# Attention over memory slots and a routed expert: a batch's queries, keys, values and phi laid on 128 partitions, scores on 16 array tiles, and the opening in another order

## The chip, the core and the metric

The kernel runs on one core of one Trainium2 chip. The core has a matrix engine (PE, with its weight loads shown apart as PEld), a vector engine (DVE), an activation engine (ACT), a general engine (POOL), a queue engine (SP) that issues most transfers, and 16 DMA engines. SBUF is the working memory of 128 partitions; PSUM is the matrix engine's output memory, 8 banks of 512 floats a partition. The metric is the device time of one execution in microseconds (us), taken as the median of several runs.

## The reference, cut to what matters

```python
# q, k, v: [8, 8, 576, 64]   phi: [8, 8, 576, 32]   (batch, head, token, ...)
a = softmax(phi over its 32 memory slots)
k_m, v_m = a^T k, a^T v                  # [8, 8, 32, 64]: 32 memory slots per head
attn = softmax(q k_m^T / 8)              # over the 32 slots
x = (attn v_m), heads side by side       # [4608, 512]
logits = x w_gate + modality_bias[modality_id]
e = argmax(logits); gate = softmax(logits)[e]
out = gate * (relu(x w1[e]) w2[e])       # w1: [8, 512, 1024], w2: [8, 1024, 512]
```

## The kernel before

**The work.** The attention never forms x. Since x w1 = attn (v_m w1), the kernel multiplies the 32 value rows of each head into the first expert matrix once per batch (`value_weights`, L604; two halves of 512 columns) and then takes attn times that product as the hidden layer. Large products are taken in a fast 32-bit form with each operand split into a rounded upper part and a remainder; three products (upper by upper, upper by remainder, remainder by upper) stand for one. That gives three matmul lines in `hidden` (L617 to L619) and three terms in `outputs` (L643). One expert is guessed for all tokens from the first token's modality (`guess`, L180); `others` and `verdict` check the guess, and `again` holds the general way, which doesn't run here.

**Per batch** the attention does, in this order: `mem_max`, `mem_top`, `mem_exp` (softmax weights over phi's slots with a shared maximum; DVE, two PE transposes, ACT), `kv_products` and `kv_divide` (L317, L343: keys and values of the slots, and the sums that divide them), `mem_turn` (keys and values transposed through PE, copied out by ACT), `mem_gate` (L421: values times the gate weights), `q_turn` (L432: queries transposed in 32 by 32 blocks by DVE, in place), `scores` (L442), `soften` and `normalise` (softmax over slots, on DVE and ACT), `a_split` (attention weights as upper part and remainder) and `logits`, `gate`. The experts then do `hidden` in two parts per batch (tokens in 4 and 5 of 9 groups), `outputs` for tiles of 128 tokens, and the store.

**Layout.** A batch's 576 tokens are 64 row blocks of 9. Queries lie in `q_sb` with a pair of batches, one on each half of the 128 partitions, all 8 heads side by side. For keys, values and phi a row block is cut in two pieces of 5 and 4 tokens, which lie on neighbouring partitions (`load_keys`, L158); the shorter piece is padded by a column of zeros, or of a very low number for phi. So `kv_products` contracts 128 partitions in 5 steps, for each of two head groups g and four heads j: 40 matmuls on array tiles of 128 rows by 32 columns. `scores` works on one batch's half of the partitions, in two parts: 32 matmuls of 32 by 32 tiles per part, on two of the four row groups of the array. (A matmul of plain 32-bit floats is two rows in the trace: 40 matmuls of the code stand as 80.)

**What sets the order.** Each engine runs its own instructions in program order. `weave` (L903) writes that order: two lists, attention steps and expert steps, each step with the steps that it needs, a due time, and a table of assumed costs (`TAKES`, L688). It takes an attention step when it is due and its inputs should be ready, else the next expert step. All waits are semaphores put in by the framework.

**The opening** is written out in `plan_first` (L745) and at L958 to L989: phi, queries, keys and values of batch 0 are loaded, the matrix engine is kept going by matmuls on zeros (`warm`, L146; 38 at the start, then 4, 26, 6, 6, 3 and 3), and the chain for part 0 of batch 0 runs to its `a_split` (step x0), behind which `hidden` starts. The first half of w1 and of w2 are loaded behind the guess.

**PSUM.** Four banks (`pe`) rotate among the expert products; one bank each is named `pa` and `mem`; two are `sc`, for scores.

Of the kernel before, what the change touches and what calls it, by code (L numbers as in the profile page):

```python
# [53 lines left out]

@with_exitstack
def attn_moe(ctx: ExitStack, tc: tile.TileContext, q, k, v, phi, mod_id, w_gate, mod_bias, w1, w2, out):
    nc = tc.nc
# [7 lines left out]
    KC = 5  # L65
# [15 lines left out]
    LOW = -1e30  # L81
# [11 lines left out]
    def bank(name):  # L93
        return (ps_e if name == "pe" else ps_x).tile([P, 512], F32, name=name)
# [9 lines left out]
    kTs = [const.tile([P, NG, 2, P], F32, name=f"kT{i}") for i in range(4)]  # L104
# [13 lines left out]
    q_sb = big.tile([P, H, QC * D], F32, name="q_sb")  # L118
    kv_sb = big.tile([P, 2, H, KC * D], F32, name="kv_sb")
    phs = [big.tile([P, H, KC * M], F32, name=f"ph{i}") for i in range(2)]  # L120
    raw1 = big.tile([P, KCH, FF], F32, name="raw1")

    raw2 = kv_sb.rearrange("p t h x -> p (t h x)")[:, 0:FCH * DM].rearrange("p (c d) -> p c d", d=DM)
# [29 lines left out]
    def rows_in(src, b, half):  # L153
        r0, r1 = (KC, QC) if half else (0, KC)
        n = src.shape[3]
        return src[b].rearrange("h (p c) d -> p h (c d)", c=QC)[:, :, r0 * n:r1 * n]

    def load_keys(dst, src, b):  # L158

        n = src.shape[3]  # L160
        nc.sync.dma_start(dst[1::2, :, n:KC * n], rows_in(src, b, 1))
        nc.sync.dma_start(dst[0::2, :, :], rows_in(src, b, 0))

    def load_phi(b):
        load_keys(phs[b % 2], phi, b)

    def load_kv(b, t):
        load_keys(kv_sb[:, t], (k, v)[t], b)

    def first_bias():  # L170

        mine = wk.tile([P, E], F32, name="mine")
        live["mine"] = mine
        for m in range(NMOD):
            if m == 0:
                nc.vector.tensor_scalar(mine, mb[:, m], is_m0[m], None, op0=ALU.mult)
            else:
                nc.vector.scalar_tensor_tensor(mine, mb[:, m], is_m0[m], mine, op0=ALU.mult, op1=ALU.add)

    def guess():  # L180

        mine = live.pop("mine")
# [3 lines left out]
        nc.vector.tensor_reduce(fstar, mine, axis=AX.X, op=ALU.max)  # L186
# [53 lines left out]
    def load_queries(pair):  # L240
        for i in range(2):
            nc.sync.dma_start(
                q_sb[QP * i:QP * (i + 1)], q[2 * pair + i].rearrange("h (p c) d -> p h (c d)", c=QC)
            )

    def load_first_queries(b):

        src = q[b].rearrange("h (p c) d -> p h (c d)", c=QC)
        for part in range(2):
            half, c0, n = lies(b, part)  # L250

            (nc.scalar if b == 0 and part else nc.sync).dma_start(
# [856 lines left out]
```

## Time and profile before

| | us |
|---|---|
| median of 3 runs | 421.99 (421.29 to 422.07) |
| the profiled execution's own time | 422.38 |
| its span | 420.6 |
| first matmul of `hidden` (start) | 30.91 |
| first matmul of `outputs` (start) | 39.10 |

The span runs from the first to the last instruction of the profiled execution; 1.8 us of that execution lie around it. A row of the timeline gives start, duration, engine, line, operation, tiles and, in brackets, how long the engine stood idle before it and what ended that. Rows of the same kind next to each other are merged, with their count behind an x. A row of the table of stages (windows) gives the stretch, its length, busy time of PE, PEld, DVE, ACT and POOL with instruction counts, the granted PE clock (1.00 is full speed), the share of the DMA engines' time in use, and GB/s. Ends of matmuls are modelled, so costs on PE are best read from one start to the next.

### The profile page before, as it was taken

The page shows a single profiled execution, that of the slowest core. Times are in us where ns is not written, and L with a number is a line of the kernel's source. Part 1 is how long each engine was busy: PE and PEld are TensorE (multiplying, and loading weights), DVE is VectorE, ACT ScalarE, POOL GpSimd, SP SyncE. Part 2 cuts the span into 40 slices and gives each one's busy share as a digit, 9 for nine tenths or more (in the row PEclk, how much of TensorE's full clock was granted, in tenths as well). Part 3 has the DMA queues.
Part 4 walks back from the last instruction along what each step waited for, and adds up shares of the span by engine and source line. Part 5 has one row for each costly group of instructions (what it writes and reads, how often), then busy time and mean ns, then how long its engine had stood idle before and what let it go on. Part 6 is the DMA issues. An engine that isn't in the chain of part 4 may idle for free.

```text
span 420.6 us, 10080 instructions
## 1 busy us (share of the span) xinstructions
PE 399.8 (95%) x4224; PEld 324.0 (77%) x4224; DVE 243.4 (58%) x575; ACT 150.0 (36%) x355; POOL 36.2 (9%) x66
## 2 busy tenths in 40 slices
PE   8599979999999999999999999999999999989993
PEld 6458877688858979697967878688877889778982
DVE  4566875873778436864685425884588406861400
ACT  1156243433433334442432424343342423431410
POOL 2047400002000200002000200002000200000000
PEclk9869999999999999999999999999999999999998
DMA  7999267983611299617311289431701011341112
GB/s 177 325 351 295 50 164 223 201 306 94 240 27 38 71 295 206 251 27 220 114 27 27 83 286 215 178 100 43 235 13 38 26 27 28 126 152 26 27 27 56
DMA packets 42167, 56.91 MB, mean 135 GB/s; under 512 B 3712, under 2 KB 30336, under 8 KB 42112
## 3 DMA queue, kind: packets, MB, share of 16 engines
q1 hardware_dynamic: 41296, 55.51, 45.4%
q10 hardware_dynamic: 816, 0.66, 0.6%
q8 instruction: 35, 0.57, 0.6%
q14 instruction: 20, 0.16, 0.1%
HBM read 37.29 MB, written 18.87 MB: 134 GB/s over the span
## 4 chain that ended last, share of the span: by engine, by line
PE 86%; DVE 5%; DMA 4%; ACT 3%; issue 1%; ACTq 0%; DVEq 0%
PE pe L643 47%; PE pe L617 8%; PE pe L618 7%; PE pe L619 7%; PE sc L452 5%; PE mem L327 4%; PE pe L594 4%; DMA q_sb<-in_q_dram 3%; PE pa L537 2%; PE mem L138 1%; ACT exp L303 1%; DMA mb<-n_moe_modality_bias_dram 1%; PE pa L150 1%; DVE hl L626 1%; DVE vwl L144 1%
## 5 line engine op out<-in xcount | busy, mean ns | idle before, releaser
L643 PE MATMUL pe<-w2h,hh 128*128 128x512 f32 x288 | 118.2, 411 | 0.0
L643 PE MATMUL pe<-w2h,hl 128*128 128x512 f32 x288 | 112.4, 390 | 0.0
L643 PE MATMUL pe<-w2l,hh 128*128 128x512 f32 x288 | 110.5, 392 | 0.0
L626 DVE SCALAR_TENSOR_TENSOR hl<-pe,hh 128x256 fp32r<-128x256 f32 (+2 forms) x160 | 58.3, 393 | 55.0 <-ACT hh L623 54.3
L643 PEld LDWEIGHTS pe<-w2h,hh 128*128 128x128 f32 x288 | 54.0, 188 | 23.1 <-issue 13.3
L623 ACT ACTIVATE hh<-pe 128x256 fp32r<-128x256 f32 (+2 forms) x160 | 52.9, 362 | 40.3 <-PE pe L619 39.9
L643 PEld LDWEIGHTS pe<-w2l,hh 128*128 128x128 f32 x288 | 54.0, 188 | 12.1
L643 PEld LDWEIGHTS pe<-w2h,hl 128*128 128x128 f32 x288 | 54.2, 188 | 9.2
L656 ACT ACTIVATE ob<-pe,gates 128x512 f32<-128x512 f32 x36 | 24.7, 689 | 71.8 <-PE pe L643 47.7
L617 PE MATMUL pe<-xbh,vwh 128*128 128x320 f32 x128 | 40.1, 313 | 1.6 <-DVE hl L626 1.6
L617 PE MATMUL pe<-xah,vwh 128*128 128x256 f32 x128 | 37.5, 293 | 2.6 <-DVE hl L626 1.8
L618 PE MATMUL pe<-xbl,vwh 128*128 128x320 f32 x128 | 39.5, 309 | 0.0
L619 PE MATMUL pe<-xbh,vwl 128*128 128x320 f32 x128 | 39.5, 309 | 0.0
L618 PE MATMUL pe<-xal,vwh 128*128 128x256 f32 x128 | 36.3, 283 | 0.6 <-DVE xal L144 0.6
L619 PE MATMUL pe<-xah,vwl 128*128 128x256 f32 x128 | 36.1, 282 | 0.0
L267 POOL TENSOR_TENSOR t2sums<-exp 128x512 f32<-128x512 f32 x6 | 7.7, 1284 | 271.1 <-ACT exp L303 271.1
L617 PEld LDWEIGHTS pe<-xah,vwh 128*128 128x128 f32 x128 | 24.4, 191 | 4.9 <-DVE hl L626 2.7
L486 ACT ACTIVATE a<-a 128x640 f32<-128x640 f32 (+2 forms) x17 | 11.2, 657 | 46.5 <-DVE a L485 46.5
L435 DVE STREAM_TRANSPOSE q_sb<-q_sb 128x512 f32<-128x512 f32 (+2 forms) x34 | 23.3, 729 | 4.8 <-DMA q_sb<-in_q_dram 4.8
L617 PEld LDWEIGHTS pe<-xbh,vwh 128*128 128x128 f32 x128 | 24.1, 188 | 2.6 <-DVE hl L626 2.3
L618 PEld LDWEIGHTS pe<-xal,vwh 128*128 128x128 f32 x128 | 24.5, 191 | 1.1 <-DVE xal L144 0.8
L619 PEld LDWEIGHTS pe<-xah,vwl 128*128 128x128 f32 x128 | 24.4, 191 | 0.0
(114 smaller groups left out, 478.5 us busy)
## 6 DMA issues: line engine op xcount, KB each, us to landing
out_dram<-ob SPq DMA_DIRECT2D x64, 128.0 KB, 2.4
q_sb<-in_q_dram SPq DMA_DIRECT2D x6, 1152.0 KB, 11.0
kv_sb<-in_k_dram SPq DMA_DIRECT2D x8, 640.0 KB, 5.9
kv_sb<-in_v_dram SPq DMA_DIRECT2D x8, 640.0 KB, 8.0
kv_sb<-in_k_dram SPq DMA_DIRECT2D x8, 512.0 KB, 5.1
kv_sb<-in_v_dram SPq DMA_DIRECT2D x8, 512.0 KB, 7.0
ph<-in_phi_dram SPq DMA_DIRECT2D x8, 320.0 KB, 3.6
ph<-in_phi_dram SPq DMA_DIRECT2D x8, 256.0 KB, 3.3
```

The lines of the kernel that those rows point to most:

```text
L327: nc.tensor.matmul(kvp[M * j:M * (j + 1), g, :, :], lhsT=pe[:, h, c * M:(c + 1) * M], rhs=kv_sb[:, ts.start:ts.stop, h, c * D:(c + 1) * D] ...
L435: nc.vector.transpose(x, x)
L452: nc.tensor.matmul(to[M * j:M * (j + 1), a], lhsT=kTs[b % 4][p0:p0 + BL, g, u, M * j:M * (j + 1)], rhs=qT[p0:p0 + BL, NG * j + g, c0:c0 + ...
L486: nc.scalar.activation(x, x, AF.Exp, scale=SCALE)
L594: nc.tensor.matmul(pvs[g][M * j:M * (j + 1), :], lhsT=vT[b][rows, j, :], rhs=raw1[rows, j, cols], start=True, stop=True, tile_position=(D ...
L617: nc.tensor.matmul(ph[:, 0:n], lhsT=vh[:, g, cols], rhs=xh, start=(g == 0), stop=False)
L618: nc.tensor.matmul(ph[:, 0:n], lhsT=vh[:, g, cols], rhs=xl, start=False, stop=False)
L619: nc.tensor.matmul(ph[:, 0:n], lhsT=vl[:, g, cols], rhs=xh, start=False, stop=(g == NG - 1))
L623: nc.scalar.activation(hs[0][:, f, h0:h0 + p1 - p0], ph[:, p0:p1], AF.Relu)
L626: nc.vector.scalar_tensor_tensor(hl, ph[:, p0:p1], 0.0, hh.bitcast(F32), op0=ALU.max, op1=ALU.subtract)
L643: nc.tensor.matmul(po, lhsT=tile_columns(hl if n == 1 else hh, f, t), rhs=(w2l if n == 2 else w2h)[:, f, :], start=(f == n == 0), stop=(f ...
L656: nc.scalar.activation(ob, po, AF.Copy, scale=gate_of(b, t))
```

## The change

**Layout.** Queries, keys, values and phi of one batch now lie on 128 partitions: the lower half holds heads of group 0, the upper half those of group 1, with the 64 row blocks of 9 tokens in each half. One transfer fills a tensor of a batch (`halves`); the padding and its fills are gone; `q_sb` is two buffers that take batches in turn.

**Scores** of a whole batch (from batch 1 on) are one step: 32 matmuls of 288 columns, on all four row groups and four column groups of the array, each row group writing its own bank. The four banks are the two pairs `pair0` and `pair1`, into which `pa`, `mem` and `sc` have been merged: `pair0` serves warm matmuls, logits and now `mem_gate`, `pair1` the rest of the memory steps. So scores take both pairs. Batch 0 keeps two steps, of 128 and 160 columns.

**Keys and values:** `kv_products` contracts 64 partitions in 9 steps on tiles of 64 rows by 32 columns, the two head groups side by side: 72 matmuls in place of 40. `mem_top` has one transpose in place of two; `mem_exp` spreads the maximum by two matmuls on 64 columns of the array in place of two transposes; `keys_out` is one ACT copy in place of two or four; the sums of batch 1 go from DVE to POOL, as those of batches 2 to 7 already did.

**Opening:** loads go phi, keys, first 4 query groups, values, last 5 query groups, modality ids, gate weights; then the guess and w1, w2. The values' products of batch 0 are split in two steps, the split of the value weights into upper (ACT) and lower (DVE) steps, and the first four blocks of `hidden` are taken in two passes (two terms, then the third), so that they don't need the lower part at once.

```diff
-    kTs = [const.tile([P, NG, 2, P], F32, name=f"kT{i}") for i in range(4)]
+    kTs = [const.tile([P, 2, P], F32, name=f"kT{i}") for i in range(2)]
...
+    def halves(src, b):
+        return src[b].rearrange("(j g) (p c) d -> (g p) j (c d)", g=NG, c=QC)
     def load_phi(b):
-        load_keys(phs[b % 2], phi, b)
+        nc.sync.dma_start(phs[b % 2], halves(phi, b))
...
-    def kv_products(b, ts, name="mem"):
+    def kv_products(b, ts, banks=None, cs=range(QC)):
...
-            for c in range(KC):
-                for j in range(HG):
-                    h = NG * j + g
+        for c in cs:
+            for j in range(HG):
+                for g in range(NG):
+                    half = slice(QP * g, QP * (g + 1))
                     nc.tensor.matmul(
-                        kvp[M * j:M * (j + 1), g, :, :], lhsT=pe[:, h, c * M:(c + 1) * M],
-                        rhs=kv_sb[:, ts.start:ts.stop, h, c * D:(c + 1) * D],
-                        start=(c == 0), stop=(c == KC - 1), tile_position=(0, M * j),
+                        kvp[g][M * j:M * (j + 1)], lhsT=pe[half, j, c * M:(c + 1) * M],
+                        rhs=kv_sb[half, ts.start:ts.stop, j, c * D:(c + 1) * D],
+                        start=(c == 0), stop=(c == QC - 1), tile_position=(QP * g, M * j),
                     )
...
-    def scores(b, part):
-        half, c0, n = lies(b, part)
-        sc = ps_x.tile([P, 2, 512], F32, name="sc")
-        qT = q_sb.rearrange("p h (c u t) -> p h c u t", u=2, t=BL)
-        for g in range(NG):
-            to = sc[:, :, g * n * BL:(g + 1) * n * BL].rearrange("p a (c t) -> p a c t", t=BL)
-            for u in range(2):
-                for j in range(HG):
-                    for a in range(2):
-                        p0 = QP * half + BL * a
+    def scores(b, c0=0, n=QC):
+        sc = [pair_of_banks(g) for g in range(NG)]
+        qT = q_sb[b % 2].rearrange("p j (c u t) -> p j c u t", u=2, t=BL)
+        cs = slice(c0, c0 + n)
+        for u in range(2):
+            for j in range(HG):
+                for g in range(NG):
+                    for a in range(2):
+                        p0 = QP * g + BL * a
                         nc.tensor.matmul(
...
+                            sc[g][M * j:M * (j + 1), a, c0 * BL:(c0 + n) * BL].rearrange("p (c t) -> p c t", t=BL),
+                            lhsT=kTs[b % 2][p0:p0 + BL, u, M * j:M * (j + 1)], rhs=qT[p0:p0 + BL, j, cs, u, :],
+                            start=(u == 0), stop=(u == 1), tile_position=(p0, M * j),
                         )
...
     def mem_gate(b):
-        pg = bank("mem")
+        pg = bank("pa")
...
-        "s0": (1.05, ""), "s1": (1.25, ""), "e": (0.0, "D1.3 A0.45"), "n": (0.0, "D2.8"),
+        "s0": (0.75, ""), "s1": (0.9, ""), "s": (1.3, ""), "e": (0.0, "D1.3 A0.45"), "n": (0.0, "D2.8"),
...
-        nothing(26)
+        nothing(22)
...
-        add(("x", 0, 0), "x0", [("n", 0, 0, 2)], a_split, 0, 0)
-        add(("vw", 0, 1), "vw", [], value_products, 0, 1, floor=20.7)
-        add(("vws", 0, 1), "nothing", [], value_split, 1)
+        add(("vwu", 0, 0), "vwu", [("vw", 0, 0)], value_upper, 0)
+        add(("vw", 0, 1), "vwp", [], value_products, 0, 1, pair_(1), floor=19.7)
+        add(("x", 0, 0), "x0", [("n", 0, 0, 2)], a_split, 0, 0)
+        add(("vwl", 0, 0), "vwl", [("vwu", 0, 0)], value_lower, 0)
+        add(("vwu", 0, 1), "vwu", [("vw", 0, 1)], value_upper, 1)
+        add(("vwl", 0, 1), "vwl", [("vwu", 0, 1)], value_lower, 1)
...
-                if t == 2 and f == FCH - 1 or t == 3 and f == FCH // 2 - 1:
+                if t == 2 and f == (FCH // 2 if b else FCH) - 1 or t == 3 and f == FCH // 2 - 1:
                     next_values(t - 2)
```

The first place is SP's queue at the start of the program. Before (`ph` is phi, `kv_sb` keys and values, `raw_105` w1; the last query piece of batch 0 is issued from ACT and isn't in this list):

```order
L161 DMA ph_103<-in_phi_dram 64x8x128
L162 DMA ph_103<-in_phi_dram 64x8x160
L252 DMA q_sb<-in_q_dram 64x8x256
L161 DMA kv_sb<-in_k_dram 64x8x256
L162 DMA kv_sb<-in_k_dram 64x8x320
L161 DMA kv_sb<-in_v_dram 64x8x256
L162 DMA kv_sb<-in_v_dram 64x8x320
L188 TENSOR_LOAD star
```

The same place now:

```order
L159 DMA ph_102<-in_phi_dram 128x4x288
L162 DMA kv_sb<-in_k_dram 128x4x576
L166 DMA q_sb_99<-in_q_dram 128x4x256
L162 DMA kv_sb<-in_v_dram 128x4x576
L166 DMA q_sb_99<-in_q_dram 128x4x320
L957 DMA mid<-in_moe_modality_id_dram 64x8x18
L961 DMA wg<-in_moe_w_gate_dram 128x4x8
L190 TENSOR_LOAD star
```

Seven transfers of 64 partitions became five of 128, keys went ahead of the first queries, and modality ids and gate weights, which stood behind w1, went ahead of the guess (`star`).

The second place is PE from the keys' transposes to the scores of batch 1 (`L643` and `L623` are output products, `vT` the transposed values, `wgd` the gate weights). Before:

```order
L138 MATMUL mem<-ident,keys 128x128 x2
L138 MATMUL mem<-ident,values 128x128
...
L643 MATMUL pe<-w2l,hh 128x512
L452 MATMUL sc<-q_sb,kT_78 32x128 x32
L424 MATMUL mem<-wgd,vT_82 32x16 x4
L452 MATMUL sc<-q_sb,kT_78 32x160 x32
```

Now:

```order
L623 MATMUL pe<-w2l,hh 128x512
L140 MATMUL pair_1059<-ident,keys 128x128 x2
L140 MATMUL pair_1059<-ident,values 128x128
L397 MATMUL pair_1066<-wgd,vT_80 32x16 x4
L420 MATMUL pair_1072<-q_sb_100,kT_78 32x288 x2
L420 MATMUL pair_1073<-q_sb_100,kT_78 32x288 x2
```

The nine output products between the transposes and the scores are gone in this batch, `mem_gate` stands ahead of the scores instead of between them, and it writes the pair of banks that the scores need next. The row of x2 then alternates between the two pairs, 16 rows in all.

The third place is DVE around that point in batch 1. Before:

```order
L435 STREAM_TRANSPOSE q_sb<-q_sb 128x2x256 x4
L435 STREAM_TRANSPOSE q_sb<-q_sb 64x8x64
L429 COPY vg_89<-mem 128x2x8
L478 STREAM_TRANSPOSE a<-sc 128x512
L483 TENSOR_REDUCE mx<-a 128x16
```

Now:

```order
L408 STREAM_TRANSPOSE q_sb_100<-q_sb_100 128x576 x4
L402 COPY vg_87<-pair_1066 128x2x8
L447 STREAM_TRANSPOSE a<-pair_1072 128x256
L447 STREAM_TRANSPOSE a<-pair_1073 128x256
L451 TENSOR_REDUCE mx<-a 128x16
```

The four query transposes stand ahead of the copy (`vg`) that empties the pair for the scores, and the reading of the scores is two instructions in place of one.

More of the change, by code (lines that the diff above doesn't have):

```diff
@@ L64, in attn_moe @@
     BL = 32
-    KC = 5
     QP, QC = 64, 9
@@ L206, in guess @@
             else:
-                raw = wk.tile([P, H, 2 * M], F32, name="t2sums").rearrange("p h x -> p (h x)")
+                raw = wk.tile([P, HG, 4 * M], F32, name="t2sums").rearrange("p h x -> p (h x)")
             nc.sync.dma_start(raw, second[:, c])
@@ L212, in prepare @@
     def prepare():
+        for t in [wgd] + vg:
+            nc.gpsimd.memset(t, 0.0)
         for r in range(2):
@@ L289, in mem_exp @@
     def mem_exp(b):
-        ph = phs[b % 2]
+        ph = phs[b % 2].rearrange("p j (c m) -> p j c m", m=M)
         topc = live["topc", b]
-        pe = wk.tile([P, H, KC * M], F32, name="exp")
+        pe = wk.tile([P, HG, QC * M], F32, name="exp")
+        px = pe.rearrange("p j (c m) -> p j c m", m=M)
         pb = bank("mem")
         for g in range(NG):
-            turn(pb[:, g * P:(g + 1) * P], topc[:, g:g + 1].broadcast_to([P, P]))
-        for g in range(NG):
-            peak = pb[:, g * P:(g + 1) * P].rearrange("p (h o m) -> p h o m", h=HG, o=1)
-            part = pe[:, g::NG].rearrange("p h (c m) -> p h c m", c=KC)
+            nc.tensor.matmul(
+                pb[QP * g:QP * (g + 1), 0:P], lhsT=topc[:, g:g + 1].broadcast_to([P, QP]), rhs=ident,
+                start=True, stop=True, tile_position=(0, QP * g),
+            )
@@ L331, in kv_products @@
                     )
         if ts.start == 0:
-            psum = pk[:, NG * 2 * D:]
-            for g in range(NG):
-                for j in range(HG):
+            for j in range(HG):
+                for g in range(NG):
+                    half = slice(QP * g, QP * (g + 1))
                     nc.tensor.matmul(
-                        psum[M * j:M * (j + 1), g:g + 1], lhsT=sums[:, NG * j + g, :], rhs=ones_c,
-                        start=True, stop=True, tile_position=(0, M * j),
-                    )
@@ L340, in kv_products @@
-            live["psum"] = psum
-        live["kvp"] = kvp
+                        pk[g][M * j:M * (j + 1), n * D:n * D + 1], lhsT=sums[half, j], rhs=ones_c[half],
+                        start=True, stop=True, tile_position=(QP * g, M * j),
+                    )
     def kv_divide(b, ts):
@@ L751, in nothing, with turns, pair_ @@
             add(("nothing", len(attention)), "nothing", [], warm, n)
-        add(("max", 0), "max", [], mem_max, 0, floor=6.2)
-        add(("first",), "first", [], first_bias)
+        def turns(part, k, floor):
+            add(("qt", 0, part, k), f"qt{part}", [], q_turn, 0, RA * part, rows_of(part), slice(2 * k, 2 * k + 2), floor=floor)
+        def pair_(i):
+            return lambda: [x[:, g] for x in [pair_of_banks(i)] for g in range(NG)]
+        add(("first",), "nothing", [], first_bias)
@@ L767, in plan_first @@
-        turns([0])
-        add(("sums", 0), "sums", [("exp", 0)], mem_sums, 0)
-        add(("k", 0), "k", [("exp", 0)], kv_products, 0, range(1), floor=12.6)
-        turns([1])
+        turns(0, 0, 9.6)
+        add(("sums", 0), "first sums", [("exp", 0)], mem_sums, 0)
+        turns(0, 1, 9.6)
+        add(("k", 0), "k", [("exp", 0)], kv_products, 0, range(1), floor=8.5)
         add(("kn", 0), "kn", [("k", 0), ("sums", 0)], kv_divide, 0, range(1))
-        turns([2, 3])
-        nothing(6)
+        v = range(1, 2)
@@ L803, in step @@
         def step(part):
-            if b or part == 0:
-                add(("s", b, part), f"s{part}", [("kvT", b), turns_of(b, part)], scores, b, part)
-            for k in range(3):
-                before = ("e", b, part, k - 1) if k else ("s", b, part)
+            for k in range(4):
+                before = ("e", b, part, k - 1) if k else ("s", b, part if b == 0 else 0)
                 add(("e", b, part, k), f"e{part}{k}", [before], soften, b, part, k)
```

384 lines of the change are left out of this document (183 added, 201 removed), and 20 rows, old and new, of the table TAKES.

## The prediction

> **What bounds the kernel now.** I read the page's busy times and chain first.
>
> ```profile
> PE 399.8 (95%) x4224; PEld 324.0 (77%) x4224; DVE 243.4 (58%) x575; ACT 150.0 (36%) x355; POOL 36.2 (9%) x66
> PE 86%; DVE 5%; DMA 4%; ACT 3%; issue 1%; ACTq 0%; DVEq 0%
> ```
>
> PE holds 86% of the chain that ends last. So a change pays if it takes time out of PE's row of work, or lets that row begin earlier. Next the timeline of the opening, up to the first output product; the chain of waits runs along these rows.
>
> ```profile
> 1.10 7.23 PE L150 MATMUL pa<-busy 128*128 128x256 bf16 x38 [1.10 <-POOL busy L966]
> 7.02 0.69 DVE L267 TENSOR_TENSOR t2top<-ph 128x512 f32<-128x512 f32 x1 [4.54 <-DMA ph<-in_phi_dram]
> 11.02 1.47 ACT L303 ACTIVATE exp<-exp 128x640 f32<-128x640 f32 x2 [5.80 <-DVE exp L299]
> 15.60 1.32 PE L327 MATMUL mem<-kv_sb,exp 128*32 128x64 f32 x80 [2.73 <-DMA kv_sb<-in_k_dram]
> 16.55 0.71 DVE L435 STREAM_TRANSPOSE q_sb<-q_sb 128x512 f32<-128x512 f32 x1 [4.83 <-DMA q_sb<-in_q_dram]
> 18.33 0.42 DVE L312 TENSOR_TENSOR sums<-sums,exp 128x256 f32<-128x256 f32 x1
> 18.90 0.39 PE L336 MATMUL mem<-ones_c,sums 128*32 128x1 f32 x16 [1.98 <-DVE sums L312]
> 19.80 0.63 ACT L360 ACTIVATE keys<-mem,rec 128x128 f32<-128x128 f32 x2 [7.32 <-DVE rec L348]
> 21.21 1.53 ACT L394 COPY kT<-mem 64x256 f32<-64x256 f32 x4 [0.78 <-PE mem L138]
> 22.38 1.96 PE L452 MATMUL sc<-q_sb,kT 32*32 32x128 f32 x64
> 24.45 0.45 DVE L478 STREAM_TRANSPOSE a<-sc 128x256 f32<-128x256 f32 x1 [3.54 <-PE sc L452]
> 29.34 0.77 DVE L510 STREAM_TRANSPOSE aT<-a 128x256 f32<-128x256 f32 x2
> 30.22 0.63 ACT L143 CAST xah<-aT 128x512 fp32r<-128x512 f32 x1
> 30.91 0.38 PE L617 MATMUL pe<-xah,vwh 128*128 128x256 f32 x1 [0.75 <-ACT xah L143]
> 31.93 0.38 PE L618 MATMUL pe<-xal,vwh 128*128 128x256 f32 x1 [0.64 <-DVE xal L144]
> 39.10 0.40 PE L643 MATMUL pe<-w2h,hh 128*128 128x512 f32 x1
> ```
>
> The exponentials are done at 12.49, but keys land at 15.6 and queries at 16.55. The first query transpose blocks DVE for 4.83 us, the sums stand behind it, and PE's sums behind them. The stages by microsecond show what that does to the clock.
>
> ```profile
> 14.00:15.00 1.00, 0.00 (x0) 0.00 (x0) 0.00 (x0) 0.00 (x0) 0.00 (x0) 1.00 1.08 265
> 16.00:17.00 1.00, 0.92 (x67) 0.76 (x55) 0.45 (x1) 0.00 (x0) 0.00 (x0) 1.00 1.08 349
> 20.00:21.00 1.00, 1.00 (x7) 0.61 (x5) 0.91 (x2) 0.43 (x2) 0.00 (x0) 0.50 1.01 377
> 26.00:27.00 1.00, 1.00 (x27) 0.67 (x19) 0.93 (x3) 0.56 (x3) 0.35 (x2) 0.50 1.04 387
> 28.00:29.00 1.00, 0.97 (x22) 0.37 (x29) 0.90 (x4) 0.03 (x1) 0.94 (x4) 1.00 1.03 387
> ```
>
> Behind PE's two gaps (2.73 and 1.98 us) the granted clock is 0.50, and 1.00 again at 28 us: the first scores ran 64 rows in 1.96 us. The DMA engines are full throughout.
>
> Third, the steady part, where PE is almost never idle. Batch 2:
>
> ```profile
> 100.20 2.39 PE L327 MATMUL mem<-kv_sb,exp 128*32 128x128 f32 x80
> 102.40 0.28 PE L336 MATMUL mem<-ones_c,sums 128*32 128x1 f32 x16
> 112.90 0.39 PE L643 MATMUL pe<-w2h,hl 128*128 128x512 f32 x1
> 113.12 0.39 PE L643 MATMUL pe<-w2l,hh 128*128 128x512 f32 x1
> 113.44 1.15 PE L452 MATMUL sc<-q_sb,kT 32*32 32x128 f32 x64
> 114.53 0.50 PE L643 MATMUL pe<-w2h,hh 128*128 128x512 f32 x1
> 114.86 0.40 PE L643 MATMUL pe<-w2h,hl 128*128 128x512 f32 x1
> 117.83 0.39 PE L643 MATMUL pe<-w2l,hh 128*128 128x512 f32 x1
> 118.15 1.32 PE L452 MATMUL sc<-q_sb,kT 32*32 32x160 f32 x64
> 119.40 1.09 PE L594 MATMUL pe<-raw,vT 64*32 64x512 f32 x16
> ```
>
> and the places where PE waits longest in the two batches behind the opening:
>
> ```profile
> 53.56 0.44 PE L138 MATMUL mem<-ident,topp 128*128 128x128 f32 x2 [0.95 <-DVE topp L277]
> 61.09 0.42 PE L617 MATMUL pe<-xbh,vwh 128*128 128x320 f32 x1 [1.59 <-DVE hl L626]
> 65.06 3.07 DVE L435 STREAM_TRANSPOSE q_sb<-q_sb 128x512 f32<-128x512 f32 x5
> 70.66 0.17 DVE L429 COPY vg<-mem 128x16 f32<-128x16 f32 x1 [2.53 <-PE mem L424]
> 71.56 1.32 PE L452 MATMUL sc<-q_sb,kT 32*32 32x160 f32 x64 [0.97 <-PE mem L424]
> ```
>
> **Scores, seven batches.** From the last output product before to the first after, less the 0.23 us that one product takes of itself (112.90 to 113.12), the first part costs 114.53 − 113.12 − 0.23 = 1.18 us, and about 0.1 more since the next start follows after 0.33; the second 119.40 − 117.83 − 0.23 = 1.34, and 0.1. Together 2.7 us a batch. Inside, a row starts every (114.53 − 113.44)/64 = 17.0 ns at 128 columns and 19.5 ns at 160: 0.078 ns a column on 8 tiles, and a fixed 7 ns. Now there are 64 rows of 288 columns. If 16 tiles run side by side the column price halves: 7 + 288 × 0.039 = 18.2 ns, 1.17 us, with one entry and exit (0.2) 1.37. If no more than 8 run, 7 + 22.5 = 29.5 ns, 1.89 + 0.2 = 2.09. I take the first, since the price per column fell with tiles so far: kv's rows (4 tiles) go from 16.5 ns at 64 columns (15.60, 1.32 us) to 27.5 at 128 (100.20 to 102.40), 0.17 ns a column, twice that of 8 tiles. Gain 1.3 × 7 = **−9**, bounds −9.3 and −4.3.
>
> **Keys and values, seven batches.** 80 rows took 2.20 us. Now 144 rows on 8 tiles. The nearest row of 128 columns on 8 tiles is the scores' 17.0 ns: 2.45 us, +0.25 a batch, **+1.7**. Low end 16.5 ns (2.38 us, +1.2). High end: the two halves don't overlap, 144 × 27.5 = 3.96 us, +12.3. Against that end stands L594, on the same 64 by 32 tiles: 16 rows of 512 columns in 1.02 us (119.40 to 120.42), 64 ns or 0.125 ns a column, well under 0.17. [...]
>
> The transposes and matmuls of the maximum, and the fewer copies on ACT, I count at nothing: one transpose less a batch is near 0.1 us of PE, two changes of tile shape in `mem_exp` may take it back; ACT is at 36%.
>
> **Waits behind the opening.** The 0.95 at 53.56 should go: DVE has the maximum of batch 1 earlier against PE, since the part before it no longer stands behind x (below). The 1.59 at 61.09 arose with the sums of batch 1 between DVE's remainders; they go to POOL, idle there. The 0.97 at 71.56 stays in another form: the scores need `pair0`, which `vg` must empty, and `vg` stands on DVE behind four query transposes, some 3.3 us (3.07 for five smaller ones). In batch 1 PE has nine output products (2.1 us), transposes and `mem_gate` (0.6) between the sums and the scores, DVE 0.4 + 3.3 + 0.2 = 3.9: a wait of 1.2; in batch 2, with three more products, 0.5. Later batches have 3 to 6 products more, about no wait. Softmax steps, logits and gate stand behind on DVE; hidden needs them only a batch's length later. So −2.5 + 0.7 = **−1.8**, bounds −4 and +3.
>
> **The opening.** A packet price first: at 265 GB/s (packets of 1 to 1.3 KB, 14 us) one of 16 engines takes 69 ns for about 1.15 KB; at 377 to 387 GB/s (2 KB rows of w1 and w2) 85 ns. That is some 45 ns plus 0.02 ns a byte. Batch 0's phi goes from 1024 packets of 512 and 640 B to 512 of 1152 B, keys and values from 1024 of 1 and 1.25 KB each to 512 of 2.25 KB.
>
> ```profile
> raw<-in_moe_w_dram SPq DMA_DIRECT2D x2, 1024.0 KB, 13.2
> ```
>
> Estimates of landings, 512 packets over 16 engines from 3.5 us on: phi 5.7 (7.0 before), keys 8.6 (15.6), first queries 10.6 (16.55), values 13.5, last queries 15.7, ids and gate weights some 18, the halves of w1 20.9 and 23.6 (before, issued at 11.3 and 12.0 and 13.2 us later, about 25 on average). The chain: the 38 warm matmuls still hold PE until 8.33, so the maximum isn't turned before; before, 5.5 us lay between phi (7.02) and the end of the exponentials (12.49); this takes back most of phi's 1.3, but the pieces are a tenth smaller: about 11.7. Keys' 144 rows at 16.5 ns from 12.0 end at 14.4; the sums on DVE, 1.5 us before (17.26 to 18.75) and now four steps, some 1.7, at 13.4; the sums on PE at 14.8 (19.3 before). The first part of values, now ahead of the keys' transposes, ends at 16.1; transposes 0.5; one copy of 0.4 in place of 1.53: 17.1; scores of 64 rows at about 17 ns at full clock: 18.2, against 24.4 (22.38 + 1.96). With PE's gaps gone I expect the clock to stay at 1.00. From scores to aT is DVE and ACT work that isn't changed, 24.45 to 30.11, so 23.9; xah 24.5. The value weights need the second half of w1 (23.6) and 1.0 us: 24.6. So `hidden` begins near 24.7 and runs freely from about 25.5 (31.93 before). From there to the outputs its blocks and the second scores took 7.2 us; these scores save 64 × (19.5 − 13.2 ns) = 0.4, and a new wait of some 0.6 comes in, because they need `pair1`, which DVE empties last. Outputs at about 33.0: **−6**. If only w1 counts, −2.7; if everything falls well, −8. The gain is kept after that: the first outputs' third term needs w2's remainders, which POOL had ready by 46.8:
>
> ```profile
> 45.51 1.30 POOL L674 TENSOR_TENSOR w2l<-t2sums,w2h 128x512 fp32r<-128x512 f32 x1
> ```
>
> The same packets as before make w2, behind a w1 some 3 us earlier, and the ids, on which POOL's work before it hangs, come ahead of w1; so these remainders move by 3 us or more, and the third term has 7.5 us of two-term products ahead of it.
>
> **Sum.** −9 + 1.7 − 1.8 − 6 = −15.1. Against the profiled execution (422.38, of it 420.6 span and 1.8 around, unchanged) 407.3; that execution lies 0.4 above the median 421.99, so **407**.
>
> **The rivals.**
> *Only eight tiles run at once.* For it: no row here shows more than 8 side by side. Against: twice the tiles halved the price once. The scores then gain 4.3 in place of 9: 411.7. Chance 0.14.
> *The opening is bound by bytes.* DMA is full from 3 us on, and bytes ahead of w1 are the same, plus ids and gate weights in small packets. If packets don't get cheaper, `hidden` starts only 2 us earlier: 411. Chance 0.14.
> *The halves of keys and values don't overlap.* A row then starts every 27.5 ns as with four tiles: +12.3 in place of +1.7, 417.6. Chance 0.05. [...]
> *Slower: the shared pairs stop PE in every batch.* PE's products between sums and scores cover 2.8 to 5 us; DVE needs 3.9 there if it comes free on time. If DVE comes to the query transposes late (remainders and value splits queued ahead), all of PE waits for `vg`. From 2.2 us a batch the whole gain is gone (15.1/7); at 3 us it is +21 − 0.7: 427. Against: DVE is at 58% and had 2.53 us idle before `vg` at 70.66. Chance 0.04.
> A wash of half-gains with such waits, at 420 to 423, gets 0.02.
>
> **Forecast.** The first case has 0.61. Its own range is 402 to 412 from the bounds of the terms (opening ±3, waits −2 to +3). The range with the rivals is 400 to 416; it leaves out the third and the fourth. About 0.2% (0.8 us) is what a measurement of this kernel can tell from none. Faster 0.94 (all cases but the last two), same 0.02, slower 0.04.
>
> **What would show it.** Right: scores of a batch as one run of 64 rows in about 1.2 us; keys and values 144 rows in about 2.4; `hidden` at 24 to 26 us and outputs at 32 to 34; clock 1.00 through 17 to 28. Wrong: 1.9 us for the scores (eight tiles); 3 us or more for keys and values; clock 0.50 again behind a gap near 12 us; PE idle before the scores on DVE's `vg` in more than two batches, or `hidden` waiting for w1.

## The result and the profile after

The changed kernel takes **410.51 us** (410.01 to 410.68, 4 runs) beside 422.03 (421.29 to 423.44, 4 runs) for the kernel before: ratio 0.972, 95% interval 0.969 to 0.975. The profiled execution took 410.64, its span 408.9. So 11.5 us went, where 15.1 were forecast. The page's busy times and its chain:

```profile
PE 390.9 (96%) x4350; PEld 312.4 (76%) x4350; DVE 238.7 (58%) x581; ACT 143.7 (35%) x342; POOL 39.6 (10%) x79
PE 87%; DVE 3%; ACT 3%; issue 3%; DMA 2%; POOL 1%; SPq 0%; ACTq 0%; POOLq 0%
```

DVE's and DMA's shares of the chain fell; "issue", time in which an engine waited for nothing that the profile shows, went from 1% to 3%. The timeline shows where (L310 is keys and values, L319 the sums, L561 the value weights, L594 `hidden`, L623 `outputs`):

```profile
11.73 1.66 PE L310 MATMUL pair<-kv_sb,exp 64*32 64x64 f32 x144
13.54 0.24 PE L319 MATMUL pair<-ones_c,sums 64*32 64x1 f32 x8
17.66 0.23 PE L319 MATMUL pair<-ones_c,sums 64*32 64x1 f32 x5 [3.87 <-issue]
18.00 0.16 DVE L327 TENSOR_SCALAR den<-pair 128x2 f32<-128x2 f32 x1 [3.98 <-PE pair L319]
...
28.28 3.87 PE L561 MATMUL pair<-raw,vT 64*32 64x512 f32 x32
32.07 0.58 PE L594 MATMUL pe<-xah,vwh 128*128 128x256 f32 x1
39.95 0.40 PE L623 MATMUL pe<-w2h,hh 128*128 128x512 f32 x1
```

Keys ran earlier than forecast (end 13.4, forecast 14.4), and the sums began at 13.54. Then PE stood for 3.87 us with 8 of 16 sum rows done, though their inputs were ready. `hidden` began at 32.07 in place of 30.91 and outputs at 39.95 in place of 39.10: the opening, which was to give 6 us, lost 0.85. The chain of waits names a second such gap, 31 rows into the first scores:

```profile
13.54 0.24 PE pair L319 x5
13.78 3.87 issue
...
21.21 0.74 PE pair L420 x31
21.95 1.95 issue
23.89 0.86 PE pair L420 x33
```

and the windows show the clock (the column ahead of DMA share and GB/s) fall behind the first and come back at 33 us; at half clock (0.50 from 17 to 33 us) the value weights took the 3.87 us above, 2.08 before:

```profile
15.00:16.00 1.00, 0.00 (x0) 0.00 (x0) 0.00 (x0) 0.00 (x0) 0.00 (x0) 1.00 1.30 224
16.00:17.00 1.00, 0.00 (x0) 0.00 (x0) 0.00 (x0) 0.00 (x0) 0.35 (x3) 0.58 0.97 338
33.00:34.00 1.00, 1.00 (x9) 1.00 (x9) 1.00 (x3) 1.00 (x3) 0.12 (x1) 0.88 1.07 396
```

So all that was gained lies behind the opening: from first outputs to the end 381.5 us before (420.6 − 39.10), 369.0 now. Three groups of the steady part, each with the row that follows, whose start ends it (the maximum of batch 2, scores of batch 3, keys and values of batch 4):

```profile
98.02 0.44 PE L274 MATMUL pair<-ident,topc 128*64 128x128 f32 x4
98.39 0.41 PE L594 MATMUL pe<-xbh,vwh 128*128 128x320 f32 x1
...
147.70 1.60 PE L420 MATMUL pair<-q_sb,kT 32*32 32x288 f32 x64
149.24 0.50 PE L623 MATMUL pe<-w2h,hh 128*128 128x512 f32 x1
...
186.35 2.25 PE L310 MATMUL pair<-kv_sb,exp 64*32 64x128 f32 x144
188.56 0.50 PE L623 MATMUL pe<-w2h,hh 128*128 128x512 f32 x1
```

PE's waits behind 40 us, before and then after (in total, times, longest; L582 and L549 are the verdict on the guess at the end, in both):

```profile
PE pe L617 <- DVE hl L626: 3.4, 4, 1.6
PE pa L582 <- DVE bad L580: 1.1, 1, 1.1
PE sc L452 <- PE mem L424: 1.0, 1, 1.0
PE mem L138 <- DVE topp L277: 0.9, 1, 0.9
PE mem L424 <- ACT vT L405: 0.2, 1, 0.2
```

```profile
PE pair L397 <- ACT vT L378: 1.2, 1, 1.2
PE pair L549 <- DVE bad L547: 1.1, 1, 1.1
PE pair L420 <- DVE vg L402: 0.6, 2, 0.3
PE pe L623 <- DVE hl L606: 0.4, 2, 0.2
PE pair L319 <- POOL sums L253: 0.3, 1, 0.3
PE pe L594 <- DVE hl L606: 0.2, 1, 0.2
```

### The profile page after: what moved, and what is told of

It reads as the page before. It is cut to its first block, busy times and chain, and to the rows that moved or that the text cites. A ratio compares the mean times of both kernels' runs of the same rounds, so it can differ in the third digit from the quotient of the medians.

```text
span 408.9 us, 10298 instructions
## 1 busy us (share of the span) xinstructions
PE 390.9 (96%) x4350; PEld 312.4 (76%) x4350; DVE 238.7 (58%) x581; ACT 143.7 (35%) x342; POOL 39.6 (10%) x79
## 4 chain that ended last, share of the span: by engine, by line
PE 87%; DVE 3%; ACT 3%; issue 3%; DMA 2%; POOL 1%; SPq 0%; ACTq 0%; POOLq 0%
PE pe L623 49%; PE pe L594 23%; PE pe L561 4%; PE pair L420 3%; PE pair L310 3%; DMA q_sb<-in_q_dram 2%; PE pair L508 1%; PE pair L140 1%; DVE hl L606 1%; ACT exp L283 1%; ACT hh L603 1%; ACT ob L636 1%; PE pair L561 0%; PE pair L152 0%; PE pair L274 0%
## 5 line engine op out<-in xcount | busy, mean ns | idle before, releaser
L623 PE MATMUL pe<-w2h,hh 128*128 128x512 f32 x288 | 117.9, 409 | 0.4 <-DVE hl L606 0.4
L623 PE MATMUL pe<-w2h,hl 128*128 128x512 f32 x288 | 112.5, 390 | 0.0
L623 PE MATMUL pe<-w2l,hh 128*128 128x512 f32 x288 | 110.4, 391 | 0.0
L623 PEld LDWEIGHTS pe<-w2h,hh 128*128 128x128 f32 x288 | 54.0, 188 | 25.3 <-issue 12.9
L623 PEld LDWEIGHTS pe<-w2l,hh 128*128 128x128 f32 x288 | 54.0, 188 | 12.0
L623 PEld LDWEIGHTS pe<-w2h,hl 128*128 128x128 f32 x288 | 54.2, 188 | 9.4
L636 ACT ACTIVATE ob<-pe,gates 128x512 f32<-128x512 f32 x36 | 24.7, 689 | 82.6 <-PE pe L623 41.9
L594 PE MATMUL pe<-xbh,vwh 128*128 128x320 f32 x128 | 39.8, 311 | 0.0
L594 PE MATMUL pe<-xbl,vwh 128*128 128x320 f32 x128 | 39.6, 309 | 0.0
L594 PE MATMUL pe<-xbh,vwl 128*128 128x320 f32 x128 | 39.5, 309 | 0.0
L594 PE MATMUL pe<-xah,vwh 128*128 128x256 f32 x128 | 37.1, 292 | 0.2 <-DVE hl L606 0.2
L594 PE MATMUL pe<-xal,vwh 128*128 128x256 f32 x128 | 36.2, 285 | 0.1
L594 PE MATMUL pe<-xah,vwl 128*128 128x256 f32 x128 | 35.3, 283 | 0.0
L249 POOL TENSOR_TENSOR t2sums<-exp 128x512 f32<-128x512 f32 x7 | 9.0, 1286 | 262.2 <-ACT exp L283 262.2
L594 PEld LDWEIGHTS pe<-xah,vwh 128*128 128x128 f32 x128 | 24.7, 193 | 3.0 <-ACT xah L488 1.7
L447 DVE STREAM_TRANSPOSE a<-pair 128x256 f32<-128x256 f32 (+1 forms) x32 | 13.6, 461 | 21.3 <-PE pair L420 21.3
L594 PEld LDWEIGHTS pe<-xal,vwh 128*128 128x128 f32 x128 | 24.6, 192 | 0.6 <-DVE xal L491 0.3
L594 PEld LDWEIGHTS pe<-xbh,vwh 128*128 128x128 f32 x128 | 24.1, 188 | 0.5 <-issue 0.2
L594 PEld LDWEIGHTS pe<-xbl,vwh 128*128 128x128 f32 x128 | 24.1, 188 | 0.3
L594 PEld LDWEIGHTS pe<-xah,vwl 128*128 128x128 f32 x128 | 24.0, 191 | 0.3 <-issue 0.3
```

The lines of the kernel that those rows point to most:

```text
L249: eng.tensor_tensor(t2, src[:, :, 0:4 * M], src[:, :, 4 * M:8 * M], op=op)
L447: nc.vector.transpose(a[:, g].rearrange("p a c m -> p a (c m)"), sc[g][:, :, RA * part * BL:(RA * part + n) * BL])
L594: nc.tensor.matmul(ph[:, 0:n], lhsT=(vl if k == 2 else vh)[:, g, cols], rhs=xl if k == 1 else xh, start=(g == k == 0), stop=(g == NG - 1 a ...
L623: nc.tensor.matmul(po, lhsT=tile_columns(hl if n == 1 else hh, f, t), rhs=(w2l if n == 2 else w2h)[:, f, :], start=(f == n == 0), stop=(f ...
L636: nc.scalar.activation(ob, po, AF.Copy, scale=gate_of(b, t))
```

## The experiments

**What stops PE in the opening.** Two readings of the 3.87 us. The next step in PE's order is the first part of the values: PE's queue could have reached ahead to it and stood there until the values landed. Or the instructions were not there yet. Against the first speaks the trace of the changed kernel itself: the values landed at 14.0 us, 3.6 us before PE went on. For the second speaks a DMA queue of its own in the page of the changed kernel (packets, MB, share), and its one packet in each of two windows, 15 to 16 and 21 to 22 us:

```profile
q8 instruction: 36, 0.59, 0.6%
...
q8 instruction: 1, 0.02, 7.7%
q8 instruction: 1, 0.02, 6.6%
```

0.59 MB in 36 packets is 16.4 KB each. Up to the first gap PE ran 38 + 1 + 4 + 4 + 22 + 144 + 8 = 221 matmul rows, up to the second 8 + 80 + 2 + 6 + 31 = 127 more. Every row has a weight load; with these and the few other instructions of PE in the trace the gaps lie behind 449 and 705 instructions, 256 apart. Each gap ends 2.5 to 2.7 us after such a packet began (15.0 and 21.4). Below, a *piece* is what one such packet brings, and an *edge* the place in PE's program where a piece ends. That a piece is 256 instructions of PE is an estimate from these counts: 256 lie between the gaps, and the 36 packets stand beside 8780 instructions of PE in the trace, 34.3 times 256.

The first run moves the values' first step away from the sums:

```diff
-        add(("v", 0, 0), "v1", [], kv_products, 0, v, two_banks, range(RB), floor=12.8)
         ...
         add(("e", 0, 0, 0), "e", [("s", 0, 0)], soften, 0, 0, None, 0)
+        add(("v", 0, 0), "v1", [], kv_products, 0, v, two_banks, range(RB))
         add(("v", 0), "v2", [], kv_products, 0, v, None, range(RB, QC))
```

> The changed kernel with the first values' step moved from ahead of the keys' transposes to behind the first scores. In the changed kernel PE stands for 3.87 us in the middle of the 16 rows of sums (8 done at 13.78, the next at 17.66). Theory A, instructions come late: PE's program arrives in pieces of about 128 matmul rows with their weight loads, and the piece is in a transfer that ends near 15 us and is used some 2.5 us later; what stands behind the sums doesn't matter, so PE still stops 8 or 9 rows into the sums, until 17.3 to 18.0, stops again some 128 rows later (now in the values, not in the scores), the first scores are read by DVE at 21.5 to 22.5 in place of 24.78, and the time is 408 to 410.5. Theory B, the values' transfer: PE's queue reaches ahead to the values' step and stands there until the values land; then the gap in the sums is gone, DVE adds to the sums at about 14 in place of 18.0, the first outputs come at 34 to 36.5 in place of 39.95, and the time is 404 to 407.

```profile
17.73 0.28 PE L319 MATMUL pair<-ones_c,sums 64*32 64x1 f32 x8 [3.87 <-issue]
27.40 1.62 PE L310 MATMUL pe<-kv_sb,exp 64*32 64x64 f32 x97 [3.85 <-issue]
```

The gap stands where it stood, after 8 rows and for 3.87 us, with nothing behind it that waits for the values. The next comes 8 + 2 + 6 + 64 + 47 = 127 rows on, now in the values. That rules out the values' transfer as the cause. The time, 412.26 (412.11 to 414.31; ratio 0.977, 0.971 to 0.983), was above what theory A gave: the second gap became 3.85 us and fell on the values, so `hidden` began at 34.59.

The second and third put more rows ahead of keys and values (220 small warm matmuls and a few large ones in place of the 38); the third moves the values' step too and takes warm matmuls of 512 columns.

```diff
-        warm(BUSY)
+        warm_rows(220, 128)   # 128 columns on tiles of 128 by 32, four side by side
+        warm(8)               # third run: warm(4), of 512 columns
```

> The changed kernel with the 38 opening warm matmuls replaced by 220 small ones of about the same total time (32 output columns of the array, 128 wide) and 8 of the old kind; nothing else is moved. Theory A, instructions come late, in pieces of 128 rows that are asked for when the piece before last is used up: 190 rows more ahead of keys and values put the edge of a piece elsewhere. No stop in the sums, DVE adds to the sums at 13.8 to 14.6 in place of 18.0; PE stops instead some 50 to 60 rows into the first values' step, until 18 to 19, and the keys' transposes behind it stay at 18.5 to 20, so the time stays within 1.5 of 410.5. Theory B, the values' transfer holds up PE's queue: the gap stays in the sums, until 17.3 to 18.0.

> Both edits together, and the other warm matmuls half as many and twice as wide, so that the edge of a piece of instructions falls behind the first scores. Theory A: no stop longer than 0.7 us from 11.7 us to the end of the first scores, which end at 16 to 17.5 in place of 24.7; clock 1.00 at least to 18 us; from there w1 (landing 21 to 23.5) holds the value weights; outputs begin at 33 to 36, time 403.5 to 407. Theory B gives 404 to 407 here as it does for the first of these runs; if that one keeps its gap and this one loses it, it is the instructions.

```profile
10.64 1.23 PE L152 MATMUL pair<-busy 128*128 128x256 bf16 x5 [3.38 <-issue]
24.34 0.65 PE L318 MATMUL pe<-kv_sb,exp 64*32 64x64 f32 x22 [4.60 <-issue]
33.04 0.68 PE L318 MATMUL pe<-kv_sb,exp 64*32 64x64 f32 x31 [3.87 <-issue]
```

The gap left the sums, as forecast, and came 58 rows into the values. But PE had stopped already among the warm matmuls, after 223 rows at 7.26 us, until 10.64. I had the place of the edges right, and not that 220 rows would be used up long before the next piece could be there. Times: 418.19 (416.77 to 420.06; ratio 0.989, 0.983 to 0.996) and, for the third, 414.03 (413.69 to 415.74; 0.980, 0.974 to 0.985), which stopped four times, 8.4 us in all, 126 to 128 rows apart. The second run was forecast within 1.5 us of 410.5, the third at 403.5 to 407: both missed.

Why does a piece take some 6 us (PE went on at 17.66 and, after the second gap, at 23.89)? In the next kernel the guess, and so w1 and w2, is moved behind the keys' transposes, so that the DMA engines have nothing to move from 16 to 21 us but one packet of instructions:

> The changed kernel with the guess of the expert, and so the transfers of w1 and w2, moved behind the keys' transposes; between 13 and 20 us the DMA engines then have next to nothing to move but ids and gate weights. It tells why a piece takes so long. If the piece waits behind the data of the other queue, its transfer comes within 1.5 us of the request and PE's stop in the sums shrinks from 3.87 us to 2 or less. If the delay is of the request itself, the stop stays at 3.3 to 4.4. The time gets worse either way, since w1 lands some 8 us later: 414 to 420.

```profile
17.00:18.00 1.00, 0.13 (x13) 0.13 (x20) 0.00 (x0) 0.00 (x0) 0.91 (x5) 0.50 0.00 0
18.00:19.00 1.00, 1.00 (x88) 1.00 (x85) 0.76 (x3) 0.34 (x2) 0.86 (x5) 0.50 0.09 16
```

The first gap stayed (4.15 us), which the expectation had named as the sign of a late request. But DMA was busy until past 15 us, with queries, ids and gate weights, and the packet came at 15.1, 15.0 before, so the first gap tests nothing. The second is gone. PE went on at 17.87, and the next packet began 1.0 us later (18.9), with nothing else moving around it; in the changed kernel it began 3.8 us after PE went on (17.66 to 21.4), at 385 GB/s. That speaks for a packet that waits behind the data, from one such pair. From its begin until PE goes on it takes another 2.4 to 2.8 us in these openings. What sets off the request is left open: where PE soon had to wait again for something else, the next packet came later, 7.2 us after PE went on in the first run and 6.3 in the second. The time, 411.08 in one execution, was hardly worse, against the forecast: outputs began only 1.3 us later (41.21), since the scores came 1.9 us earlier.

**Fewer rows, or earlier ones.** Keys and values of batch 0 in one run save 144 rows, but wait for the values:

```diff
-        add(("k", 0), "k", [("exp", 0)], kv_products, 0, range(1), floor=8.5)
-        add(("kn", 0), "kn", [("k", 0), ("sums", 0)], kv_divide, 0, range(1))
+        add(("k", 0), "k", [("exp", 0), ("sums", 0)], kv_products, 0, range(2))
+        add(("kn", 0), "kv", [("k", 0)], kv_divide, 0, range(2))
```

The second kernel adds 96 small warm matmuls at the start and wide ones (32-bit, 480 columns) for the others, the third has the wide ones alone.

> The changed kernel with keys and values of batch 0 taken in one run of 144 rows of 128 columns, as in all other batches, in place of 144 rows for the keys and 144 for the values (it waits for the values, which should land near 13.2 us). That takes 144 rows out of PE's program ahead of hidden. Theory A (instructions come in pieces of 128 matmul rows; the first edge lies after 221 rows; a piece is asked for when the one before last is used up, about row 93, and is there some 6 us after): rows ahead of keys and values are the same, so PE still stops after about 8 of the 16 rows of sums, now at 15.3, until 18.8 to 20.2, and then not again up to the end of the first scores, which end at 22.2 to 23.8 in place of 24.7; the values need no time of their own, so outputs begin at 36.5 to 38.5 in place of 39.95, time 407 to 409.5. Theory A2 (the piece comes at a fixed time, whatever PE does): the stop ends at 17.7, scores at 21, time 405 to 407.

> The same with the warm matmuls of another form: 96 small ones at the very start, the others few and wide (plain 32-bit floats, 480 columns), so that the request of the first piece falls near 4 us and only some 342 rows stand ahead of the end of the first scores, less than the second edge at 349; the three wide ones behind the scores keep PE going until w1 lands. Theory A: no stop over 0.7 us up to the end of the first scores, at 17.3 to 18.8; clock 1.00 to there; hidden begins at 24.5 to 27, outputs at 33 to 35.5, time 403 to 406. If requests don't follow the count of rows, a stop of 3 us or more stays and the time is 407 or more.

> As the one before without the 96 small matmuls (wide ones in their place), so that there are few rows and the request comes late, in the middle of keys and values. Theory A: PE runs through the sums and stops 28 to 40 rows into the 64 of the first scores, until 19 to 20.8; scores end 1.5 to 3 us later than in the one before; outputs at 34 to 37.5, time 404.5 to 407.5.

First the rows of the first of the three kernels, then of the second, then of the third.

```profile
14.21 3.29 PE L310 MATMUL pair<-kv_sb,exp 64*32 64x128 f32 x143 [2.26 <-DMA kv_sb<-in_v_dram]
20.81 0.28 PE L319 MATMUL pair<-ones_c,sums 64*32 64x1 f32 x8 [3.27 <-issue]
```

```profile
15.57 3.84 PE L316 MATMUL pair<-kv_sb,exp 64*32 64x128 f32 x144 [2.93 <-DVE q_sb L414]
24.50 5.46 PE L151 MATMUL pair<-busy 128*128 128x480 f32 x6 [0.51 <-DVE a L453]
```

```profile
21.59 0.68 PE L426 MATMUL pair<-q_sb,kT 32*32 32x128 f32 x32 [1.73 <-issue]
189.72 0.26 PE L325 MATMUL pair<-ones_c,sums 64*32 64x1 f32 x13 [1.93 <-issue]
```

The stops came where the count put them: after 8 sum rows until 20.81 (forecast 18.8 to 20.2; not the fixed 17.7 of A2), none at all with the early rows, and 32 rows into the scores without them, until 21.59 (forecast 19 to 20.8). The times were not as forecast: 413.90 (ratio 0.978, 0.975 to 0.982), 410.12 (405.92 to 410.84; 0.967, 0.963 to 0.971) and 412.01 (0.974, 0.970 to 0.977). Two reasons. The values landed at 14.1, 15.4 and 14.0 us; in the first two kernels PE idled 2.26 and 2.93 us ahead of keys and values, which then took 3.29 and 3.84 us in place of 2.2 (mostly at half clock, an estimate from these times), and in the second the three wide matmuls behind the scores took 5.46 us (six rows of 480 columns took 3.33 in the version below, so the clock had probably fallen once more) and held up the value weights; outputs began at 40.59, later than in the changed kernel, without any stop on instructions. Its fastest execution, 405.92, had a mean clock of 0.997, the others 0.979 to 0.987. And the edges of all later pieces moved as well: in the last row above PE stops at 187.8 us, in batch 4, for 1.93 us, since 160 rows of keys, values and sums pass in 2.2 us and an edge fell near their end. The first kernel had two such stops (1.24 and 1.68 us).

**Two prices, measured.** The loop over head groups outermost, in scores (8 tiles at a time) and in keys and values (4 tiles at a time):

```diff
+        for g in range(NG):
             for u in range(2):
                 for j in range(HG):
-                    for g in range(NG):
                         for a in range(2):
```

> The changed kernel with the loop over head groups outermost in the scores, so that no more than 8 tiles (two row groups) can run side by side at a time; the same 64 rows of 288 columns. In the changed kernel these take 1.53 us from the first row's start to the next product's, 23.9 ns a row. If the four row groups do run side by side (only in part, since 18.2 ns were forecast), 8 tiles cost the forecast's 29.5 ns: 1.9 us, +0.35 to +0.5 a batch, the time 413 to 414. If 23.9 ns is what 8 tiles cost and the other half brings nothing, the rows stay at 1.5 us and the time at 410.5.

> The changed kernel with the loop over head groups outermost in keys and values, so that only the four tiles of one half of the array's rows run side by side at a time; the same 144 rows of 128 columns. In the changed kernel they take about 2.0 us (13.8 ns a row, with the sums 2.21). If the two halves running side by side make that price, the rows go to the forecast's far end, 27.5 ns: 3.9 to 4.1 us, and seven batches cost 11 to 13 us more: 421 to 424. If a row simply costs 13.8 ns on tiles of 64 rows, nothing changes: 410 to 411.

```profile
148.24 1.95 PE L420 MATMUL pair<-q_sb,kT 32*32 32x288 f32 x64
150.13 0.50 PE L623 MATMUL pe<-w2h,hh 128*128 128x512 f32 x1
```

```profile
189.22 3.42 PE L310 MATMUL pair<-kv_sb,exp 64*32 64x128 f32 x132
192.93 0.50 PE L623 MATMUL pe<-w2h,hh 128*128 128x512 f32 x1
```

Scores: 1.89 us, 29.5 ns a row, the very price that the prediction gave to 8 tiles; 1.53 on 16 tiles. So taking 16 in turn does help, but it saves a fifth and not near two fifths. Whether the tiles or the two pairs of banks that they write set this limit, the run doesn't tell. Time 414.23 (411.47 to 416.18; ratio 0.981, 0.973 to 0.988), too spread to show by itself the 2.5 us that seven batches at 0.36 make. Keys, values and sums: 3.71 us in place of 2.21, some 24 ns a row (forecast far end 27.5); time 419.83 (ratio 0.995, 0.993 to 0.997; forecast 421 to 424). The halves do overlap.

**A version from this.** Merged keys and values, early small rows, and: values loaded ahead of the first queries, sums on DVE ahead of the query transposes, keys turned in the other pair of banks, wide matmuls behind the scores half as long. The second kernel moves ids and gate weights behind w1; the third is the changed kernel again, on the same chip.

```diff
         load_kv(0, 0)
-        load_queries(0, 0, RA)
         load_kv(0, 1)
+        load_queries(0, 0, RA)
```

> The opening with keys and values of batch 0 in one run, 96 small warm matmuls first and wide ones behind (as in the run of that name), and now: values loaded ahead of the first queries, the sums on DVE ahead of the query transposes, the keys' transposes into the other pair of banks so that they don't wait until the values are read out, and three wide warm matmuls of 240 columns in place of 480 behind the scores. If PE's count of rows and the values' landing are what set the opening: no stop on instructions up to the end of the first scores, which end at 17.5 to 19.5; hidden begins at 25.5 to 28, outputs at 34 to 36.5, time 404 to 407 beside 410 to 411 for the changed kernel. Rival: w1 (issued behind ids and gate weights) or the clock sets hidden's start all the same; then outputs stay at 38 to 40 and the time at 408.5 to 411.

> The same with modality ids and gate weights, whose issue holds SP for some 4 us and whose small packets halve the bytes moved near 15 us, behind w1 instead of ahead of it. If w1's landing sets hidden's start, value weights come 1.5 to 3 us earlier than in the one before and the time is 1 to 3 lower; if the chain of scores and softmax sets it, the time is the same within 0.7.

> The changed kernel as it is, on the same chip as the two before, for comparison: 410 to 411.5.

The first of these kernels, its timeline and its clock in 40 slices of the span:

```profile
13.95 2.22 PE L316 MATMUL pair<-kv_sb,exp 64*32 64x128 f32 x143 [1.35 <-DMA kv_sb<-in_v_dram]
18.59 1.23 PE L426 MATMUL pair<-q_sb,kT 32*32 32x128 f32 x64 [0.16 <-ACT kT L376]
26.10 0.39 PE L600 MATMUL pe<-xah,vwh 128*128 128x256 f32 x1 [1.62 <-ACT xah L494]
33.84 0.40 PE L629 MATMUL pe<-w2h,hh 128*128 128x512 f32 x1
...
PEclk9999999999999999999999999999999999999999
```

No stop on instructions, no fall of the clock (0.999 on average), outputs at 33.84: **403.77 us** (403.65 to 404.85; ratio 0.956, 0.953 to 0.958), beside 410.61 (410.14 to 410.93) for the changed kernel: 6.8 us, all of it in the opening (outputs began at 40.68 in the changed kernel's profile on this chip). It beats both kernels. Several edits went in together; what each of them brought is not shown. With ids behind w1 it took 405.69 (403.48 to 406.53; 0.958, 0.955 to 0.961): no gain, and the intervals overlap. In that profile the first token's bias landed 2.4 us later and the exponentials ran 1.4 us later, w1 landed no earlier (20.5 and 23.3 us; 20.5 and 23.2 in the first), and the clock fell once at 28 us (rows of `hidden` 0.21 us apart in place of 0.12; 0.991 on average). So it is no test of an earlier w1. Its two executions with a mean clock of 0.999 took 403.48, as good as the first kernel's best, 403.65.

## Why the prediction came out as it did

The time lay in the range, 3.5 us above the forecast, and in part by luck: the opening came out 6.85 us worse than forecast, and what lies behind it gained 12.5 us in place of 9.1, of which 2.0 are not placed. The mechanisms of the steady part (fewer rows for the scores, waits gone) were right, their sizes not. **The step that failed is the opening's −6**, and in it the sentence "with PE's gaps gone I expect the clock to stay at 1.00": I priced rows by their durations and never asked whether the instructions for 144 + 16 + 80 rows in some 4 us could be there. The runs put in its place: PE stops after 221 rows until the next piece arrives, and again 127 rows on. The kernel before passes the same edge at 23.3 us, 39 rows into its first scores; its packet had begun at 19.6, so PE didn't stop there. By its terms:

| term | forecast | measured | from |
|---|---|---|---|
| scores | −9 | −7.0 | 1.08 + 1.25 a batch before, 1.53 now, one change of shape fewer (0.2, the prediction's estimate): −1.0 × 7 |
| keys and values | +1.7 | −0.6 | 7 × 2.42 before; 2.72 (0.3 of it a wait that the lists hold as well) + 2.34 + 2.44 + 2.22 + 3 × 2.21 = 16.35 now |
| maximum | 0 | +0.9 | two pairs of transposes 0.27; now 0.03 + 0.37 |
| waits behind the opening | −1.8 | −3.8 | 5.5 to 2.7 by the lists; 1.7 to 0.6 inside the rows of the value weights |
| opening | −6 | +0.85 | first outputs 39.10 to 39.95 |
| not placed | | −2.0 | the rest of the span's 11.7 |

*Scores.* "The column price halves" was mis-sized: 23.9 ns a row, between my 18.2 and the 29.5 of 8 tiles. The rival of 8 tiles is out, by the run with 8.

*Keys and values.* I took the scores' 17.0 ns; the rows need 13.8 of 128 columns, and 10.1 of 64 (the 144 rows of keys start from 11.73 to 13.18). The far end lay at 24 by the run on four tiles, not at 27.5. The 160 rows with the sums took 2.21 us.

*The maximum* was not nothing: four rows on 64 columns take 0.37 us.

*Waits.* The 1.59 and the 0.95 went as forecast. The wait for `vg` was 0.3 in batches 1 and 2 (forecast 1.2 and 0.5); in batch 1 a wait for the copy of the transposed values (1.2) stands one step ahead of it. Two stops of 0.8 inside the value weights (1.82 and 1.88 us for 16 rows in place of 1.02), which I had not seen in the trace of before, are one of 0.64 now. The one now lies at an edge (behind 3009 instructions of PE), those of before do not, and their cause stays open. The slower rival, PE stopped for `vg` in every batch, did not come: from batch 3 on that wait isn't in the list.

*Opening, its pieces.* Packets did get cheaper, and the rival "bound by bytes" is out: phi landed at 6.18 (forecast 5.7), the first queries at 11.0 (10.6), values at 14.0 (13.5), the halves of w1 at 20.0 and 22.7 (20.9 and 23.6). The keys' copies, whose sums were due at 14.8, ran at 18.46. Of `hidden`'s 7.4 us of lateness (24.7 to 32.07) the two stops are 5.8. In the rest half clock (0.50) has a part: the first half of the value weights, which the chain runs through, took 2.03 in place of 1.04. The version without stops begins `hidden` at 26.10 and outputs at 33.84, near the forecast's 33.0, though its steps stand in another order. But instructions in time are not enough: the second of the merged kernels had no stop either, and its other gaps (2.93 us ahead of keys and values), with slower rows behind them (3.84 and 5.46 us), kept outputs at 40.59. So the −6 took two things for granted: instructions in time, and no other long gap of PE.

*What was listed as wrong sign* did appear: "clock 0.50 again behind a gap near 12 us", at 13.78; I had thought of a wait on data there.

## What to carry to other kernels

Where a stage runs many small instructions in a few microseconds, count them as well as timing them: here a piece of some 128 matmul rows needed about 6 us with the DMA engines full (3.8 until its packet began, 2.5 more until PE went on), once the first 220 to 223 rows were through; about 4 without other data is an estimate (1.0 and up to 2.8). The sign is a gap that ends on "issue" in the middle of a group, at a fixed count of rows, with a packet of the instruction queue that began some 2.5 us before its end; moving steps that stand behind it doesn't move it, changing the number of instructions ahead of it does. Filler that only keeps the clock up should be wide, since it uses up rows too: the version without stops has 22 wide rows beside 96 small ones, at a clock of 0.999.

## What the runs showed of the hardware

- PE's first stop came after 220 to 223 rows in nine kernels with different programs, each later edge 126 to 128 rows on. Counted in all of PE's instructions in the traces, 22 stops of these nine kernels lie behind 449 plus a multiple of 256, give or take one: 449 and 705 in the changed kernel, 961 and 1217 in the second run, 4289 at the stop in batch 4. Why the first edge lies at 449 is not shown.
- The first 16 KB packet of instructions of the changed kernel took 1.2 us of one DMA engine's time (7.7% of 16 engines in 1 us). The next one began 3.8 us after PE went on, with full DMA; in the one kernel with idle DMA there it began after 1.0.
- The same in the steady part: 1.93 us lost in batch 4, with DMA at 48 GB/s, by a shift of rows in the opening alone. So an edit can cost 2 us at a place 150 us behind it.
- Matmul rows of 64 columns on eight 64 by 32 tiles started every 10.1 ns, of 128 columns every 13.8. Rows of 288 columns cost 23.9 ns each on sixteen 32 by 32 tiles and 29.5 on eight, up to the next product's start.
